# A ring of five tiles instead of four for the transposed query factor xT

## The chip, the core and the metric

The kernel runs on one core of one Trainium2 chip. The metric is the time of one execution on the device in microseconds (us), the median of three runs. Engines are named as the profile names them: PE is TensorE's matrix multiplications, PEld its weight loads, DVE is VectorE, ACT is ScalarE, POOL is GpSimd, SP is SyncE, which issues all the transfers (DMAs) of this kernel on one queue.

## The reference

Three stages follow one another. The first is a recurrence over 768 time steps, for 4 batches and 8 heads, with a 40x40 state each. The second is a dense layer pair with an ELU between, the third a mixture of eight experts whose gate is normalised over rows and columns.

```python
for t in range(S):                                   # B, H, S, D = 4, 8, 768, 40
    y[:, :, t] = einsum('bhd,bhde->bhe', rt, state)
    Sa = einsum('bhde,bhe->bhd', state, at)
    state = state * wt[:, :, None, :] - einsum('bhd,bhe->bhde', Sa, bt)
    state = state + einsum('bhd,bhe->bhde', vt, kt)

h = x @ w_in                                         # x: 3072 x 320, w_in: 320 x 2048
g = where(h > 0, h, exp(minimum(h, 0)) - 1)
x = g @ w_out

P = exp(x @ w_gate - max)                            # 8 experts
for _ in range(8): P /= P.sum(1); P /= P.sum(0); P *= N / E
for e in range(8): out += P[:, e] * (maximum(x @ w1[e], 0) @ w2[e])
```

## The kernel before, in words

**Stages.** The recurrence is cut into 24 chunks of 32 steps. The dense layer pair works on 12 blocks of 256 rows, each in 16 units of 128 hidden columns, and a block needs the output of two chunks. The units of the dense pair are woven between the pieces of the recurrence, so both run in the first 825 us or so; the experts follow until the end, with PE multiplying nearly without a gap.

**Order.** The program order on PE, DVE, ACT and POOL is fixed by hand: two strings of tokens in `PLAN` (`order2` for the first two passes, `order` from then on) name what each pass of the loop at L1238 records, and `pin_since` chains the instructions of each engine in that order. A token such as `E2+3` in the pass c means `E2` for chunk c + 3, and `m` is one unit of the dense pair. A pass therefore works on several chunks at once: `O3b` finishes the output of chunk c - 1, `E2` and `E1` prepare chunk c + 3, `H2` and `H3` carry the recurrence over chunk c. The SP queue is not pinned, and its transfers stand in an order that the scheduler has set; it issues them one after the other, and a transfer that must wait holds up those behind it.

**The tile xT.** `E2` (L369) transposes the factor of a chunk on PE into PSUM bank 2 (L374), and ACT copies it to the tile `xT` in SBUF (L376, shown in the profile as L469, the helper `cp`). `O3b` (L585) reads that tile four passes later: DVE multiplies the chunk's output into it in place (L598), POOL duplicates its last 64 columns (L599), and SP stores it to DRAM as `yd` (L603). `xprep` (L607) loads `yd` back as `yt` (L615), and PE transposes it for the dense pair (L621). The tiles of `xT` come from the pool `r2` (on the right side of SBUF) under one tag, and they are used in turn: with a ring of four, the copy for chunk c + 3 writes into the tile of chunk c - 1, so it waits for the store L603 of chunk c - 1. In a pass of `order` the store of chunk c - 1 and the copy of chunk c + 3 belong to neighbouring tokens: `O3b+-1 ... H1 ... E2+3`.

**What stands around the copy.** On ACT, in program order: the two activations of a dense unit (L640, L641), the copy of xT, four copies of the solved values to `VU` (`H2x`, L516), then the rounding `gh` of the next unit (L649), L640 and L641 again, and the copies of `KB` (`E1`, L469). On PE: the transposes of `E2` (L374), the multiplications of `H2` (L510), a second half of a unit (L665 to L669), the first half of another (L638), the transposes of `E1` (L365), which write banks 2 and 3, and the multiplications of `H3` (L534), which read `VU`. `E1` reads the tile `KE` of the same chunk, whose one buffer is then loaded again (L315) and scaled on POOL in `prep` (L355), and `E3` (L383) reads the result on PE.

**Pairs of passes.** Every other pass also ends a triangular solve for two chunks (`tsolve`, L418): its DVE steps L445 and L452 end shortly before `O3b`, and then SP issues eight stores `Td` (L460), eight loads `TT` (L464) and one load `LT` (L408) around the store L603. In the pass between, SP has none of these to issue at that place.

Of the kernel before, what the change touches and what calls it, by code (L numbers as in the profile page):

```python
# [9 lines left out]
F32 = mybir.dt.float32  # L10
# [103 lines left out]
def build(ctx, tc, r, k, v, w, a, b, w_in, w_out, wg, w1, w2, wa_d, kb_d, re_d, ro_d, vt_d, wp_d, consts, out, C, off):  # L114
# [63 lines left out]
    r2 = rec.enter_context(tc.tile_pool(name="r2", bufs=2, side="right"))  # L178
# [178 lines left out]
    def unpad(dst, ps):  # L357
        return dst.rearrange("p (j g e) -> p j g e", j=2, g=NG), ps.rearrange("p (g x) -> p g x", g=NG)[:, :, 0:128].rearrange("p g (j x) -> p j g x", j=2)[:, :, :, 0:D]
# [9 lines left out]

    def E2(c):  # L369
        z = st[c]  # L370
        z.xT = r2.tile([128, 384], F32, tag="xT", name="xT", bufs=4)
        xv = z.xC
        for g in range(NG):
            T.transpose(PS["E2"][0][:, 128 * g:128 * g + HR], xv[0:HR, g, :], ident[0:HR, 0:HR])  # L374
        o, i = unpad(z.xT[:, 0:DM], PS["E2"][0])
        cp("XT", 0, o, i)  # L376
# [91 lines left out]
    def cp(n, i, out, in_):  # L468
        (A.copy if PLAN["eng"][n][i] == "A" else G.tensor_copy if PLAN["eng"][n][i] == "G" else V.tensor_copy)(out=out, in_=in_)  # L469
# [661 lines left out]
    with ExitStack():  # L1131
# [37 lines left out]
        mg = msteps()  # L1169
        wgen = [(k, i) for i in range(NF1) for k in "io"]  # L1170
        fns = dict(ld=loads, ldw=loadw, ldk=loadk, lu=loadv, lv=loads2, prep=prep, H1=H1, H2=H2, H3=H3, H4=H4, E1=E1, E2=E2, E3=E3, E4=E4, T=tsolve, O1=O1, O2=O2, O3a=O3a, O3b=O3b, YW=YW, LT=LT)
        done = {("ld", 0), ("ld", 1)}

# [140 lines left out]
```

## Time and profile before

| what | value |
|---|---|
| median of three runs | 2249.49 us (2245.49 to 2250.47) |
| the profiled execution's own time | 2250.63 us |
| its span, first to last instruction | 2248.8 us |
| mean granted TensorE clock | 0.964 of full speed |
| PE busy | 2137.9 us, 95% |
| PEld busy | 1934.8 us, 86% |
| DVE, ACT, POOL busy | 928.5, 815.0, 439.7 us (41%, 36%, 20%) |

The page gives shares over the whole span. Some 1420 us of it are the experts, after 825 us. The change touches the first part alone, so the stretch from 270 to 750 us, where the passes of `order` repeat, says more than the shares do. [...]

### The profile page before, as it was taken

To read this page: it belongs to the slowest core of one execution; us is meant where nothing else is said; L and a number is where in the kernel's file an instruction comes from. 1 tells how busy PE (TensorE), PEld (TensorE's weight loads), DVE (VectorE), ACT (ScalarE), POOL (GpSimd) and SP (SyncE) were. 2 spreads that over 40 slices of the span, in tenths; PEclk is the share of its full clock that TensorE was granted. 3 is DMA by queue.
4 is the path that set the end of the run, shared out by engine and by line. 5 is a ranking of instruction groups with operands and counts; after the bars stand their busy time and mean duration, and the time that the engine had idled before them with its cause. 6 is when DMAs were issued, how large, how long until landed. Compare 5 with 4: busy or idle time off the path is not lost.

```text
span 2248.8 us, 48229 instructions
## 1 busy us (share of the span) xinstructions
PE 2137.9 (95%) x20483; PEld 1934.8 (86%) x20483; DVE 928.5 (41%) x1889; ACT 815.0 (36%) x1813; POOL 439.7 (20%) x545
## 2 busy tenths in 40 slices
PE   3788999999999999999999999999999999999998
PEld 2677888999898989898888888888888888888888
DVE  6686667777766322532222222222222222222222
ACT  2344555555544565223224324223224212112111
POOL 2354333443433261002002002002002002001000
PEclk9676999999999999999999999999999999999999
DMA  6654434344442142002113112002002001000000
GB/s 161 165 161 107 114 102 100 95 110 111 105 105 72 45 122 56 29 1 56 20 20 75 23 32 78 26 27 78 27 26 65 1 1 52 1 1 20 24 24 25
DMA packets 216657, 138.50 MB, mean 62 GB/s; under 512 B 143793, under 2 KB 192306, under 8 KB 216434
## 3 DMA queue, kind: packets, MB, share of 16 engines
q1 hardware_dynamic: 216434, 135.34, 22.9%
q8 instruction: 162, 2.65, 0.5%
q14 instruction: 61, 0.50, 0.1%
HBM read 116.80 MB, written 18.48 MB: 60 GB/s over the span
## 4 chain that ended last, share of the span: by engine, by line
PE 79%; DVE 9%; DMA 4%; issue 2%; ACT 2%; SPq 2%; POOL 1%; DVEq 0%; ACTq 0%; POOLq 0%
PE h L874 28%; PE pa L918 10%; PE pa L919 10%; PE pa L917 10%; PE ph L638 5%; PE h L863 2%; PE a L665 2%; DVE Wk L452 2%; DVE Tt L445 2%; DMA yd<-xT 1%; PE P L534 1%; PE a L666 1%; PE a L667 1%; PE P L383 1%; PE P L510 1%
## 5 line engine op out<-in xcount | busy, mean ns | idle before, releaser
L878 DVE SCALAR_TENSOR_TENSOR hl<-h,hh 128x512 fp32r<-128x512 f32 x384 | 265.3, 691 | 765.9 <-ACT hh L877 765.4
L877 ACT ACTIVATE hh<-h 128x512 fp32r<-128x512 f32 x384 | 229.6, 598 | 899.2 <-PE h L874 897.5
L874 PE MATMUL h<-xs,a 128*128 128x512 f32 x2280 | 547.0, 394 | 0.2 <-DVE hl L878 0.2
L874 PEld LDWEIGHTS h<-xs,a 128*128 128x128 f32 x2280 | 421.0, 188 | 109.8 <-issue 25.4
L918 PE MATMUL pa<-a,hl 128*128 128x320 f32 x1536 | 475.8, 310 | 0.8 <-DVE hl L878 0.8
L919 PE MATMUL pa<-a,hh 128*128 128x320 f32 x1536 | 475.2, 309 | 0.0
L917 PE MATMUL pa<-a,hh 128*128 128x320 f32 x1536 | 473.9, 309 | 0.3 <-ACT logits L692 0.3
L918 PEld LDWEIGHTS pa<-a,hl 128*128 128x128 f32 x1536 | 288.9, 188 | 6.7 <-DVE hl L878 1.7
L917 PEld LDWEIGHTS pa<-a,hh 128*128 128x128 f32 x1536 | 288.6, 188 | 5.2 <-ACT logits L692 0.4
L919 PEld LDWEIGHTS pa<-a,hh 128*128 128x128 f32 x1536 | 289.0, 188 | 0.0
L825 POOL TENSOR_TENSOR a<-rw,a 128x384 fp32r<-128x384 f32 x64 | 65.2, 1019 | 1057.5 <-ACT a L823 1044.4
L638 PE MATMUL ph<-X,Wt 128*128 128x256 f32 x1536 | 234.8, 299 | 8.2 <-DVE g L647 7.8
L651 POOL TENSOR_TENSOR gl<-g,gh 128x256 fp32r<-128x256 f32 x192 | 150.1, 782 | 385.1 <-ACT gh L649 305.0
L638 PEld LDWEIGHTS ph<-X,Wt 128*128 128x128 f32 x1536 | 212.2, 205 | 13.1 <-DVE g L647 11.5
L647 DVE SCALAR_TENSOR_TENSOR g<-m,ph 128x256 f32<-128x256 f32 x192 | 79.9, 416 | 205.0 <-ACT m L641 147.9
L928 DVE SCALAR_TENSOR_TENSOR acc<-pa,Pg,acc 128x320 f32<-128x320 f32 x168 | 81.0, 544 | 184.1 <-PE pa L919 184.1
L649 ACT ACTIVATE gh<-g 128x256 fp32r<-128x256 f32 x192 | 80.1, 417 | 163.5 <-DVE g L647 162.7
L452 DVE TENSOR_TENSOR Wk<-Wk,Tt 128x132 f32<-128x132 f32 (+24 forms) x279 | 109.4, 392 | 8.6
L874 PE MATMUL h<-X,a 128*128 128x512 f32 x456 | 108.9, 394 | 0.0
L640 ACT ACTIVATE m<-ph 128x256 f32<-128x256 f32 x192 | 73.0, 380 | 89.5 <-PE ph L638 86.4
L874 PEld LDWEIGHTS h<-X,a 128*128 128x128 f32 x456 | 84.1, 188 | 21.9 <-issue 5.0
L445 DVE TENSOR_TENSOR Tt<-Wk,LT 128x132 f32<-128x132 f32 (+24 forms) x279 | 90.1, 323 | 8.0
(189 smaller groups left out, 2700.3 us busy)
## 6 DMA issues: line engine op xcount, KB each, us to landing
LT<-Ad SPq DMA_DIRECT2D x22, 512.0 KB
rw<-in_moe_w SPq DMA_DIRECT2D x64, 160.0 KB
WA<-in_wa SPq DMA_DIRECT2D x23, 422.9 KB
KE<-in_kb SPq DMA_DIRECT2D x23, 416.0 KB
rw<-in_moe_w SPq DMA_DIRECT2D x64, 128.0 KB
VU<-in_vt SPq DMA_DIRECT2D x24, 320.0 KB
raw<-in_wp SPq DMA_DIRECT2D x16, 384.0 KB
rchk<-in_wp SPq DMA_DIRECT2D x16, 384.0 KB
```

Source lines behind the costliest of these rows:

```text
L445: V.tensor_tensor(out=tv, in0=Wk[:, :, 0:ni, j:j + 1].to_broadcast(sh), in1=LT2[:, :, j, j + 1:C].unsqueeze(2).to_broadcast(sh), op=ALU.mult,)
L452: V.tensor_tensor(out=Wk[:, :, 0:ni, j + 1:C], in0=Wk[:, :, 0:ni, j + 1:C], in1=tv, op=ALU.subtract)
L638: T.matmul(ph, lhsT=Wt[0:kp, wi, 128 * f:128 * f + 128], rhs=X[0:kp, xi, :], start=(i == 0), stop=(i == 7))
L649: A.activation(out=gh, in_=g, func=AF.Copy)
L651: G.tensor_tensor(out=gl, in0=g, in1=gh.bitcast(F32), op=ALU.subtract)
L874: T.matmul(h, lhsT=a1[:, wi, :], rhs=X[bk][:, xi, :], start=(i == 0 and n == 8), stop=(i == n - 1), skip_group_check=(n == 7))
L877: dve["hh"] = A.activation(out=hh, in_=h, func=AF.Relu)
L878: V.scalar_tensor_tensor(out=hl, in0=h, scalar=0.0, in1=hh.bitcast(F32), op0=ALU.max, op1=ALU.subtract)
L917: T.matmul(o, lhsT=hh[:, ts_], rhs=a2[:, 0, :], start=(f == 0), stop=False)
L918: T.matmul(o, lhsT=hl[:, ts_], rhs=a2[:, 0, :], start=False, stop=False)
L919: T.matmul(o, lhsT=hh[:, ts_], rhs=a2[:, 1, :], start=False, stop=(f == NF2 - 1))
L928: V.scalar_tensor_tensor(out=at, in0=o, scalar=Pg[:, tt, e:e + 1], in1=at, op0=ALU.mult, op1=ALU.add)
```

## The change

One number: the tag `xT` gets five buffers. The copy for chunk c + 3 then writes into the tile of chunk c - 2.

```diff
 def E2(c):
     z = st[c]
-    z.xT = r2.tile([128, 384], F32, tag="xT", name="xT", bufs=4)
+    z.xT = r2.tile([128, 384], F32, tag="xT", name="xT", bufs=5)
     xv = z.xC
```

The order of the instructions on all five engines stays as it was, the SP queue's too. The lists of semaphores that instructions wait for differ. This is the place on ACT where chunk 11's copy stands, with what stands around it (`ph` is a PSUM tile of the dense pair, `P_101` is bank 2, `DMAHW` are the semaphores of transfers):

```order
 L640 ACTIVATE m<-ph 128x256 [waits PE_49]
 L641 ACTIVATE m<-m 128x256 [waits Activation_49]
-L469 COPY xT<-P_101 128x320 [waits DMAHW5_49,PE_49,Pool_49]
+L469 COPY xT<-P_101 128x320 [waits DMAHW3_49,PE_49]
 L516 ACTIVATE VU<-P_100 32x320 [waits DMAHW4_49,PE_49]
```

The copy still names a transfer, but another one: the store of the chunk that held the tile five chunks ago. The wait for POOL (L599 of the chunk four before) is gone. Each tile takes 1536 bytes of a partition, so the pool `r2` grows by as much.

## Rows read from the trace of the kernel before

**Rows 1.** The page: busy time, share of the span, instructions.
```profile
PE 2137.9 (95%) x20483; PEld 1934.8 (86%) x20483; DVE 928.5 (41%) x1889; ACT 815.0 (36%) x1813; POOL 439.7 (20%) x545
```

**Rows 2.** Waits of PE, 270 to 750 us: total us, times, longest.
```profile
PE P L365 <- ACT xT L469: 13.3, 6, 2.9
PE P L481 <- issue: 3.1, 2, 1.8
...
PE P L534 <- ACT VU L516: 1.0, 5, 0.2
```

**Rows 3.** Waits of ACT, 270 to 750 us.
```profile
ACT xT L469 <- DMA yd<-xT: 29.4, 7, 5.3
```

**Rows 4.** Timeline of ACT at chunk 11's copy: start, us, instruction, idle before.
```profile
331.11 0.43 ACT L469 COPY xT<-P 128x320 f32<-128x320 f32 x1 [4.57 <-DMA yd<-xT]
331.56 1.77 ACT L516 ACTIVATE VU<-P 32x320 f32<-32x320 f32 x4
```

**Rows 5.** Timeline of PE at the same place.
```profile
325.95 1.13 PE L510 MATMUL P<-RH,TT 64*64 64x40 f32 x32
...
328.07 1.12 PE L638 MATMUL ph<-X,Wt 128*128 128x256 f32 x8
331.58 0.93 PE L365 MATMUL P<-cst,KE 104*128 104x104 f32 x8 [2.40 <-ACT xT L469]
...
344.21 1.13 PE L383 MATMUL P<-aB,KE 104*64 104x64 f32 x32
```

**Rows 6.** Timeline of SP's queue, 325 to 346 us: start, us to issue, transfer.
```profile
325.30 0.61 SPq L408 DMA_DIRECT2D LT<-Ad  x1
326.01 0.54 SPq L603 DMA_DIRECT2D yd<-xT  x1
326.67 3.80 SPq L464 DMA_DIRECT2D TT<-Td  x4
...
331.02 0.46 SPq L615 DMA_DIRECT2D yt<-yd  x1
331.58 0.35 SPq L327 DMA_DIRECT2D rO<-in_ro  x1
332.55 0.33 SPq L315 DMA_DIRECT2D KE<-in_kb  x1
```

**Rows 7.** The chain that ended last: start, us, what.
```profile
0.75 4.29 DMA WA<-in_wa
...
326.01 4.99 DMA yd<-xT
...
696.75 5.00 DMA yd<-xT
```

**Rows 8.** Timeline of PE one pass later (chunk 12's copy).
```profile
360.63 1.12 PE L638 MATMUL ph<-X,Wt 128*128 128x256 f32 x8
361.59 0.88 PE L365 MATMUL P<-cst,KE 104*128 104x104 f32 x8
```

**Rows 9.** Whole passes: us, busy PE, PEld, DVE, ACT, POOL; PEclk, DMA share, GB/s.
```profile
325.51:358.07 32.56, 29.39 (x517) 27.82 (x515) 21.47 (x51) 15.70 (x41) 11.72 (x14) 0.95 0.46 125
387.56:420.33 32.77, 29.51 (x517) 27.84 (x515) 22.50 (x55) 16.15 (x42) 11.71 (x14) 0.95 0.48 129
482.90:511.34 28.44, 28.26 (x523) 27.16 (x522) 20.18 (x46) 16.85 (x44) 12.20 (x15) 1.00 0.33 77
511.34:544.51 33.17, 30.85 (x517) 29.46 (x515) 21.68 (x52) 15.91 (x41) 11.71 (x14) 0.90 0.45 124
573.33:604.09 30.76, 28.21 (x517) 26.54 (x516) 21.50 (x51) 15.72 (x41) 11.69 (x14) 1.00 0.51 135
633.21:667.02 33.81, 30.66 (x517) 29.44 (x516) 21.40 (x51) 15.79 (x41) 11.73 (x14) 0.90 0.46 121
```

**Rows 10.** The same view, stretches at half clock.
```profile
446.70:450.10 3.40, 3.40 (x19) 3.40 (x18) 0.00 (x0) 0.82 (x3) 0.73 (x1) 0.50 0.35 54
518.40:525.20 6.80, 6.61 (x82) 6.54 (x83) 1.85 (x3) 3.60 (x11) 3.46 (x4) 0.50 0.39 115
702.70:709.60 6.90, 6.90 (x89) 6.57 (x88) 0.42 (x1) 3.66 (x11) 1.46 (x2) 0.51 0.19 62
```

**Rows 11.** Timeline of POOL at the same pass.
```profile
340.76 2.35 POOL L355 TENSOR_TENSOR KE<-KE,F 104x512 f32<-104x512 f32 x2
```

## The prediction

> **What bounds the kernel now.** I read the page first: PE is busy 95% of the span and ACT 36% [rows 1]. That share mixes the experts, where PE has hardly a gap, with the first 825 us, so I asked for the waits of PE in the passes that repeat, 270 to 750 us. Most of what PE waits for there is one thing: the transposes of E1 (L365) wait six times, 13.3 us in all, for ACT's copy of xT, and H3 (L534) five times, 1.0 us in all, for the VU copies that stand behind that copy on ACT [rows 2]. The next largest item is 3.1 us at L481 without a named cause. The same view for ACT says what the copy itself waits for: the store of the tile to DRAM, 29.4 us in seven waits [rows 3]; an eighth, before 270 us, brings the profile's count to eight.
>
> Chunk 11 shows one such wait in full. The store L603 is issued at 326.01, behind the stores and loads of the solve, and lands 4.99 us later [rows 6, 7]. The copy starts at 331.11 after 4.57 us of idle ACT [rows 4]. That the store is the cause is seen twice: SP's load of yt, which needs the same store, leaves at 331.02 [rows 6]. PE has gone on meanwhile with a dense unit, until 328.07 + 1.12 = 329.19, and then stands for 2.40 us, since L365 writes the PSUM bank that the copy reads [rows 5]. One pass later there is no solve to issue, the copy does not wait, and L365 follows L638 with no gap [rows 8]. So every other pass is long: 32.56 to 33.81 us, against 28.44 us in the best short one [rows 9].
>
> A second loss comes after the wait. [...] Its price stands in the passes: the one at 573 us has the same 517 matmul records as the other long ones and a clock of 1.00, and PE is busy 28.21 us in it. In the four others PE is busy 29.39, 29.51, 30.85 and 30.66 us for the same records, at clocks of 0.90 to 0.95 [rows 9].
>
> **The change, part by part.** No instruction is added, removed or moved; the SP queue keeps its order. What goes is the wait of the copy for the newest store. It now waits for the one a pass earlier, issued some 30 us before, and that store has long landed.
>
> *Stalls of PE.* With the copy at about 326.5 us, right after L641, the VU copies (1.77 us [rows 4]) follow H2, which ends at 327.08, and are done near 328.9. PE reaches L365 at 329.19, so both its wait and that of L534 disappear: 13.3 + 1.0 = **14.3 us** [rows 2]. For the wait before 270 us I count nothing; PE is held there by another transfer.
>
> *Clock.* If PE no longer stands, I expect the half clock to go too, as in the pass at 573 us. Above 28.21 us the four passes hold 1.18, 1.30, 2.64 and 2.45 us; for the fifth, at 702 us, whose stretch is as long as that at 518 us, I take 2.5. That is **10.1 us**. The bounds are nothing (the clock drops anyway) and half of the time spent at half clock, near 13.7 us: the stretches of 6.80 and 6.90 us [rows 10], a third of 6.8 us taken for the pass at 633 us, whose clock is the same as at 511 us, and two of 3.4 us taken for the passes at 0.95 [rows 9].
>
> [...]
>
> *What is late next.* PE then runs 2.40 + 0.2 + 1.18 = 3.8 us earlier in chunk 11's pass (0.2 is a fifth of L534's 1.0). Three loads stand behind the store on SP: yt, rO, KE. SP still waits until 331.0 for the store to land before it issues yt, so they hardly move: KE can go at about 331.95 instead of 332.55 [rows 6]. POOL scales KE at 340.76 without having waited for it [rows 11], so the load took at most 340.76 - 332.55 = 8.2 us; the nearest row with a landing is WA, 4.29 us [rows 7] and nearly of the same size. With 4.29 it lands at 336.2, before POOL wants it at 340.76 - 3.8 = 337.0. With 8.2 it lands at 340.15, 3.2 us late; L383 on PE has 344.21 - 340.76 - 2.35 = 1.1 us to spare [rows 5, 11], so PE would stand 2.1 us, in six passes (chunk 23 has no such load) 12.6 us. I take the row that is nearest, WA, and count **1 us** in all for the passes where PE gains most. The yt loaded here is the second of its block; its transposes come in the second half of the pass, so it costs nothing. The solve on DVE and its stores and loads follow PE's order and move with it, so H2 finds TT as it does now.
>
> *Space.* The 1536 bytes shift the addresses of tiles; I price that at nothing, no row of the trace tells of addresses.
>
> The sum is 14.3 + 10.1 - 1 = 23.4 us. The experts start earlier by that, and as PE is the bound there, nothing fills it again. From the profiled execution, 2250.63 us, this makes 2227.2; it lies 1.1 us above the median of the runs, so I give **2226 us**. What a measurement of this kernel can tell from no change is about 0.2%, 4.5 us.
>
> **The rivals.**
>
> *The stalls go, the clock does not come back.* At 446.7 us the clock is halved for 3.40 us where no copy of xT had waited before it [rows 10]; the two nameless stalls at L481 [rows 2] show that other gaps do this too. Then 14.3 us remain: 2236 from the profiled time, 2235 for the median.
>
> *KE takes the place of the store.* SP, held by the landing of yd, is then what PE waits for by way of POOL. Priced above at 12.6 us at most: 24.4 - 12.6 = 11.8 us, 2238. It decides from a load of about 336.97 + 1.1 - 331.95 = 6.1 us on. For it speaks that the store took 4.99 us in that crowd; against it that in the short pass nothing of the kind appears [rows 8, 9].
>
> *Nothing measurable.* ACT is busy 36% and PE 95% [rows 1]; if both rivals above hold at once, 24.4 - 10.1 - 12.6 = 1.7 us are left, 2248. [...]
>
> *Slower.* [...] The stall at L481 has no cause in the profile but "issue" [rows 2], 1.3 to 1.8 us, and the clock falls after it (1.7 us for the 3.40 us of [rows 10]), so about 3.3 us each time. Should it come in each of the 14 passes between 270 and 700 us instead of two, that costs 12 x 3.3 = 39.6 us against 23.4: 2266. It decides from seven more passes on. Against it: the short passes hold no pause now, and the one at 482.9 us is busy 28.26 of 28.44 us [rows 9].
>
> That the change does not do what it says would need a tile of five chunks ago to be late too; a store that left 30 us earlier is not.
>
> **How the numbers follow.** The forecast (18 to 28 us gained) has 0.62, the clock that stays low 0.17, KE 0.07, nothing measurable 0.09, slower 0.05. All of the first three are faster by more than 0.2%: 0.86; the same 0.09; slower 0.05. The range must hold 8 in 10: the forecast with its bounds and the rival of the clock, with the KE case at its edge. Below it goes to 14.3 + 13.7 and a little for the first wait, 2220; above to the KE case and the spread of the runs, 2240.
>
> **What would show it.** In the changed kernel's profile: no row of ACT's copy waiting for yd, and none of L365 waiting for the copy; passes of some 29 us in turn, all alike; PE busy near 28.2 us in each, with a clock of 1.00. The store itself should still take 4 to 5 us, and SP still wait for it ahead of yt. Wrong I would be if L365 or L534 waited for something else at the same place, if L383 waited for POOL's KE, or if stretches at half clock were as many as before.

## The result and the profile after

The changed kernel takes 2222.78 us, the median of five runs (2220.81 to 2225.52), against 2249.49 us (2245.49 to 2254.44, five runs): 26.7 us less, a ratio of 0.988 with a 95% interval of 0.9863 to 0.9897. The profiled execution took 2223.81 us with a span of 2221.9 us. The mean granted clock of the whole span, 0.964 before and 0.976 now, says little of the change: much of the difference lies in the first 260 us, where the clock is 0.79 and 0.86 and lies anywhere between 0.79 and 0.91 in the ten profiles of this case. From 260 to 760 us it is 0.96 before and 0.98 now (columns as in [rows 9], before and then after):

```profile
260.00:760.00 500.00, 472.83 (x8362) 449.71 (x8350) 334.15 (x797) 262.50 (x674) 183.93 (x228) 0.96 0.39 99
260.00:760.00 500.00, 485.53 (x8749) 462.69 (x8746) 340.66 (x810) 276.00 (x710) 191.13 (x236) 0.98 0.40 100
```

The page's first part, which answers to [rows 1], shows PE with 15.8 us less of busy time for the same 20483 instructions. The share went from 95% to 96%, so it would have told little.

```profile
PE 2122.1 (96%) x20483; PEld 1921.1 (86%) x20483; DVE 925.3 (42%) x1889; ACT 814.1 (37%) x1813; POOL 439.4 (20%) x545
```

The waits of PE, from 270 to 740 us (columns as in [rows 2]). The rows of L365 for ACT's copy and of L534 for VU are gone, and what is left is small, apart from L481, whose stalls were there before. The 1.4 us of L621 are new:

```profile
PE P L481 <- issue: 4.9, 3, 2.1
PE P L564 <- DVE X L626: 1.9, 8, 0.5
PE ph L638 <- DVE g L647: 1.7, 7, 0.3
PE P L621 <- DVE Am L385: 1.4, 4, 0.4
...
PE P L383 <- POOL KE L355: 0.3, 1, 0.3
```

ACT's copy waits for no transfer any more in the whole span. The one row of it among the waits of ACT is for the transposes that it copies (compare [rows 3]):

```profile
ACT xT L469 <- PE P L374: 2.9, 6, 1.2
```

Chunk 11 again, now some microseconds earlier. The timeline of ACT: the copy starts at once, and the VU copies wait only 0.28 us for H2 (compare [rows 4]).

```profile
325.20 0.41 ACT L469 COPY xT<-P 128x320 f32<-128x320 f32 x1
325.89 1.78 ACT L516 ACTIVATE VU<-P 32x320 f32<-32x320 f32 x4 [0.28 <-PE P L510]
```

The timeline of PE: L638, L365 and L534 follow one another without a gap (compare [rows 5]).

```profile
326.83 1.12 PE L638 MATMUL ph<-X,Wt 128*128 128x256 f32 x8
327.79 0.88 PE L365 MATMUL P<-cst,KE 104*128 104x104 f32 x8
328.60 1.30 PE L534 MATMUL P<-VU,KB 64*40 64x40 f32 x64
...
338.53 1.15 PE L383 MATMUL P<-aB,KE 104*64 104x64 f32 x32
```

The queue of SP: the store itself is as slow as before. It leaves at 324.61, and SP issues the load of yt, which needs it, 4.98 us later (compare [rows 6]). Now only SP waits for it, with the loads that stand behind it there.

```profile
324.61 0.54 SPq L603 DMA_DIRECT2D yd<-xT  x1
...
329.59 0.34 SPq L615 DMA_DIRECT2D yt<-yd  x1
330.04 0.35 SPq L327 DMA_DIRECT2D rO<-in_ro  x1
330.43 0.37 SPq L315 DMA_DIRECT2D KE<-in_kb  x1
```

The passes (columns as in [rows 9]), a short one and then the five long ones of [rows 9]. These five of 30.76 to 33.81 us are now 28.06 to 28.82 us, at a clock of 1.00, and no longer than the short one:

```profile
295.11:324.27 29.16, 28.62 (x523) 27.10 (x522) 21.28 (x50) 16.91 (x44) 12.06 (x15) 1.00 0.35 83
324.27:352.68 28.41, 27.60 (x517) 26.30 (x515) 21.85 (x51) 15.68 (x41) 11.79 (x14) 1.00 0.52 143
...
382.37:411.19 28.82, 27.66 (x517) 26.30 (x516) 22.58 (x54) 15.85 (x41) 11.73 (x14) 1.00 0.54 143
503.23:532.00 28.77, 28.17 (x517) 26.54 (x515) 22.23 (x52) 15.72 (x41) 11.75 (x14) 1.00 0.55 143
560.96:589.42 28.46, 27.76 (x517) 26.41 (x515) 21.85 (x51) 15.72 (x41) 11.73 (x14) 1.00 0.53 144
618.61:646.67 28.06, 27.50 (x517) 26.23 (x516) 21.85 (x51) 15.72 (x41) 11.78 (x14) 1.00 0.52 146
```

The starts of these passes, set against those in [rows 9], show where the time is won. The changed kernel is 1.2 us ahead at the first long pass, 5.2, 8.1, 12.4 and 14.6 us at the next four, and 20.4 us at the end of the last.

Between 325 and 667 us one long pass is in neither list, that of chunk 15's copy. It won nothing; before, and then after:

```profile
451.44:482.89 31.45, 29.38 (x516) 27.87 (x515) 22.59 (x55) 16.06 (x41) 11.36 (x14) 0.95 0.47 130
442.72:475.43 32.71, 30.38 (x517) 28.99 (x516) 23.45 (x56) 16.17 (x42) 12.48 (x15) 0.90 0.45 126
```

There the copy had waited only 1.86 us for the store, and PE did not stand behind it at L365. So not every other pass took 32.56 to 33.81 us before, as the prediction has it: two were shorter, with 30.76 and 31.45 us.

The same view for the two places between 270 and 700 us where the clock still falls. Each stands at a stall of L481, of 1.53 us up to 437.10 and of 2.13 us up to 468.56:

```profile
436.50:440.50 4.00, 3.40 (x18) 3.35 (x19) 0.00 (x0) 0.61 (x2) 0.73 (x1) 0.61 0.28 45
467.50:475.00 7.50, 6.45 (x37) 6.36 (x38) 4.28 (x13) 1.92 (x6) 1.55 (x4) 0.54 0.23 75
```

### The profile page after: what moved, and what is told of

It reads as the page before. It is cut to its first block, busy times and chain, and to the rows that moved or that the text cites. A ratio compares the mean times of both kernels' runs of the same rounds, so it can differ in the third digit from the quotient of the medians.

```text
span 2221.9 us, 48228 instructions
## 1 busy us (share of the span) xinstructions
PE 2122.1 (96%) x20483; PEld 1921.1 (86%) x20483; DVE 925.3 (42%) x1889; ACT 814.1 (37%) x1813; POOL 439.4 (20%) x545
## 3 DMA queue, kind: packets, MB, share of 16 engines
q8 instruction: 162, 2.65, 0.5%
## 4 chain that ended last, share of the span: by engine, by line
PE 76%; DVE 13%; DMA 4%; issue 3%; ACT 2%; SPq 1%; POOL 1%; DVEq 0%; ACTq 0%; POOLq 0%
PE h L874 28%; PE pa L918 10%; PE pa L919 10%; PE pa L917 10%; PE ph L638 5%; DVE Wk L452 3%; DVE Tt L445 3%; PE h L863 3%; PE a L665 1%; DVE g L647 1%; PE P L510 1%; PE a L666 1%; PE a L667 1%; PE P L383 1%; DMA KE<-in_kb 1%
## 5 line engine op out<-in xcount | busy, mean ns | idle before, releaser
L638 PE MATMUL ph<-X,Wt 128*128 128x256 f32 x1536 | 229.8, 294 | 9.2 <-DVE g L647 8.3
L638 PEld LDWEIGHTS ph<-X,Wt 128*128 128x128 f32 x1536 | 207.4, 200 | 13.5 <-DVE g L647 10.5
```

The lines of the kernel that those rows point to most:

```text
L638: T.matmul(ph, lhsT=Wt[0:kp, wi, 128 * f:128 * f + 128], rhs=X[0:kp, xi, :], start=(i == 0), stop=(i == 7))
```

## Experiments

My theory: the copy on ACT stands until the newest store has landed, PE stands behind ACT, and the clock falls after that. The rivals were that moved addresses make the gain, that the readers on DVE and POOL hold the tile too, that the moment or the place of the copy matters in some other way, and that the store costs something besides this wait. The first four experiments start from the kernel before, the last four from the changed one.

**1. The space without the tile.** The pool grows by the same 1536 bytes, but the ring stays at four.

```diff
     def E2(c):
-        z = st[c]
+        z = st[c]; c or G.memset(r2.tile([128, 384], F32, tag="pad", name="pad", bufs=1)[:, 0:1], 0.0)
```

> Ring of four, and a tile of 1536 bytes a partition that nothing uses is added to the same pool (one memset of one column on POOL). If the wait of the copy of xT for the newest store is what the change takes away, nothing changes: about 2249 us, and the copy still waits some 32 us for the store. If the gain came from the moved addresses of the pool, the time is near 2223 us with the waits still there or shorter.

Measured: 2250.39 us, ratio 1.0002 (0.999 to 1.0014). The waits are all there. The first row below is PE's from 260 to 760 us, the second ACT's over the whole span:

```profile
PE P L365 <- ACT xT L469: 13.6, 6, 2.7
```

```profile
ACT xT L469 <- DMA yd<-xT: 33.4, 8, 5.6
```

So more space in the pool does nothing by itself. The rival of the addresses is out, as far as this one way of shifting them goes.

**2. A tile of its own for the output.** The product no longer overwrites xT, so the store holds another tile.

```diff
-        y = x if c else mt.tile([128, 384], F32, tag="yt", name="yt", bufs=2)
+        y = r2.tile([128, 384], F32, tag="yo", name="yo", bufs=2) if c else mt.tile([128, 384], F32, tag="yt", name="yt", bufs=2)
```

> Ring of four, but O3b writes its product into a tile of its own (a ring of two) and stores that one; xT is free again after the two DVE products. If it is the landing of the store that holds the tile, the copy waits for nothing and the time is that of the change, 2220 to 2227 us. If the fifth tile is needed because the readers on DVE and POOL are late too, L365 still waits for the copy and the time stays within 5 us of 2249 us. The new ring of two puts DVE's product behind the store of two chunks before, which has landed by then: nothing for that.

Measured: 2222.05 us, ratio 0.9875 (0.9856 to 0.9894), the time of the change. With a ring of four, xT is free early enough once only the DVE products read it. Neither ACT's copy nor L365 shows a wait for the tile from 260 to 760 us. The new tile takes over both the store and POOL's column copy, so this run alone does not tell which of the two held xT; in experiment 4 POOL's copy still reads xT, and the wait is gone with the store.

**3. The copy later in the pass.** One token of `order` moves; no tile is added.

```diff
-... p m E2+3 p p p p lv G prep+4 H2 m m E1+3 ldk+4 prep+4 H3 m m x prep+4 ...
+... p m p p p p lv G prep+4 H2 m m E1+3 ldk+4 prep+4 H3 m m x E2+3 prep+4 ...
```

> Ring of four, with the token E2+3 moved from before E1+3 to the place before the third step of prep, some 8 us later in each pass; no more space. If only the moment of the copy against the landing of the store matters, the store has landed by then, no engine waits for it, and the time is that of the change within 6 us: 2220 to 2230 us (the transposes and the copy may now meet other work). If the order of the two transposes in bank 2 matters more than the wait, PE waits at the new place and the time is 2235 us or more.

Measured: 2225.44 us, ratio 0.9901 (0.9883 to 0.992). Nothing waits for the store; the transposes at the new place meet the copies of KB that E1 has left to ACT in the same bank. The waits of PE from 260 to 760 us:

```profile
PE P L374 <- ACT KB L469: 1.6, 5, 0.4
```

The ring of four was too short only for the place that the copy had.

**4. The store on another queue.** From chunk 5 on, ACT issues the store.

```diff
-            SY.dma_start(out=yd[c], in_=y)
+            (A if c > 4 else SY).dma_start(out=yd[c], in_=y)
```

> Ring of four, the store of the product issued on ACT's queue from chunk 5 on instead of SP's, so that it is not behind the solve's stores and loads. If the wait is made by the place in SP's queue (the store leaves 4.5 us after its data is ready) and by the crowd of transfers there, the store leaves some 4 us earlier and lands in 2 to 3 us, the copy does not wait, and the time is 2220 to 2232 us; ACT may lose some time to its wait for POOL's last column copy. If ACT standing for that wait costs as much as the wait before, the time is 2240 us or more.

Measured: 2222.66 us, ratio 0.9888 (0.9867 to 0.991). In the timeline of ACT the store leaves at 320.66, where SP had sent it at 326.01 in a pass that began at nearly the same time [rows 6]; the copy then waits for nothing:

```profile
320.66 0.37 ACTq L603 DMA_DIRECT2D yd<-xT  x1
321.07 0.49 ACT L469 COPY RH<-P 128x160 f32<-128x160 f32 x2 [2.07 <-PE P L481]
...
325.53 0.41 ACT L469 COPY xT<-P 128x320 f32<-128x320 f32 x1
```

ACT does stand for POOL's column copy ahead of the store. Its waits from 260 to 760 us:

```profile
ACT RH L469 <- POOL xT L599: 11.5, 10, 2.0
...
ACT RH L469 <- DMA Td<-Wk: 5.1, 2, 2.7
```

These 16.6 us cost nothing that can be measured, since no row of PE's waits names the copy of RH: here a wait on ACT counted only where it reached PE. Experiments 2 to 4 remove the same wait in three other ways, and the gain of each has an interval that overlaps that of the fifth tile.

**5 to 7. Putting the delay back.** In the changed kernel, spare copies on ACT ahead of the copy of the odd chunks from 9 on: 3, 8 or 14. They write into the tile that the copy then overwrites. No transfer is involved.

```diff
-        xv = z.xC
+        xv = z.xC; [A.copy(out=z.xT[:, 0:192], in_=cst[:, 0:192]) for _ in range(3 if c > 8 and c % 2 else 0)]
```

> The change, with three spare copies of 128x192 on ACT ahead of the copy of xT for the odd chunks from 9 on (about 1 us each time, eight times; they write into the tile that the copy then overwrites). If PE has room until it reaches L365 and L534, nothing is to be seen: within 4 us of the change, 2219 to 2228 us. If the sum of ACT's work is what counts, it costs 8 us: near 2231 us.

> The same with eight spare copies, about 2.6 us each time. PE should stand for some 1.2 us at L365 and L534 together, eight times: 10 us, so near 2233 us if the clock stays, and near 2243 us if each such stall also brings the half clock.

> The same with fourteen spare copies, about 4.5 us each time, as long as the wait for the store was. If PE's stall behind the copy, and the half clock after it, made the whole difference, the time is back: 2243 to 2254 us, with L365 waiting 2 to 3 us for the copy each time and stretches at half clock after most of them. If the store itself, or its wait on SP, was part of the price, the time stays 8 us or more below that of before: under 2241 us.

Measured: 2224.31 us (ratio to before 0.9891, 0.9871 to 0.9911), 2234.54 us (0.9933, 0.9913 to 0.9954) and 2258.49 us (1.0049, 1.003 to 1.0068). Against the change that is 1.5, 11.8 and 35.7 us more. With 3 copies PE shows no row of L365 or L534 for ACT from 260 to 760 us. With 8 it shows these:

```profile
PE P L365 <- ACT xT L469: 4.8, 7, 0.8
...
PE P L534 <- ACT VU L516: 1.5, 7, 0.2
...
PE P L510 <- ACT xT L372: 1.3, 1, 1.3
```

With 14 these, and below them the spare copies themselves in ACT's timeline:

```profile
PE P L365 <- ACT xT L469: 22.4, 8, 3.1
...
PE P L534 <- ACT VU L516: 1.1, 5, 0.2
```

```profile
324.19 5.33 ACT L372 COPY xT<-cst 128x192 f32<-128x192 f32 x14
```

The delay of the copy was free at first (1.5 us of time with 3 copies) and then went into PE's time (11.8 us with 8, 35.7 us with 14). The third run missed its figure: I had taken 0.32 us for a spare copy, but fourteen take 5.33 us, 0.38 each, so the delay was longer than the wait for the store (4.57 us [rows 4]), and PE stood for 23.5 us where it had stood for 14.3 us. It shows more than a return to the old time. The time rises by 35.7 us for 23.5 us of stalls, so 12 us come on top of the stalls. The clock is enough for that. It was 0.98 from 260 to 760 us in the change; with 14 copies it is:

```profile
260.00:760.00 500.00, 464.87 (x8172) 441.51 (x8170) 330.19 (x792) 295.64 (x772) 181.52 (x223) 0.95 0.38 96
```

A mean clock lower by 0.03 over 500 us is 15 us of full-speed time, and by the trace's clock records a stretch at half clock begins within 2.3 us of the end of each of the eight stalls at L365, which last 1.5 to 3.1 us. With 8 copies this hardly shows:

```profile
260.00:760.00 500.00, 480.47 (x8536) 455.86 (x8523) 338.26 (x807) 292.71 (x759) 189.32 (x233) 0.98 0.39 99
```

The mean clock is that of the change, and of the seven stalls at L365, of 0.3 to 0.8 us, one at most is followed by a half clock. The time, 2234.54 us, is the one expected if the clock stays. The three rows make 7.6 us of stalls for 11.8 us of time; the 4 us between them are not explained.

**8. KE ahead of the store's landing.** In the changed kernel, the load of yt goes behind the load of KE on SP.

```diff
-... p p m xl p m E2+3 ... H3 m m x prep+4 ...
+... p p m p m E2+3 ... H3 m m xl x prep+4 ...
-        SY.dma_start(out=z.KE[0:HR]..., in_=kb_d[c])
+        SY.dma_start(out=z.KE[0:HR]..., in_=kb_d[c]); first["KE"] = traced()[-1].name
-                SY.dma_start(out=yt, in_=yd[2 * blk + t])
+                SY.dma_start(out=yt, in_=yd[2 * blk + t]); t and tc.add_manual_dep(traced()[-1], first["KE"], ...)
```

> The change, with the second load of yt of a block put behind the load of KE on SP (and the token xl later in the pass), so that SP does not hold KE until the store has landed. The trace of the change shows the load of KE as what ends last there, with PE waiting for it once, 0.3 us. If KE is what is late next, up to 1 us a pass is won, 7 us in all at most and nearer 1 us: 2216 to 2224 us. If the issue stalls of PE and the clock bound it instead, it is the same as the change within 4 us. If the early KE load slows the store or the loads of the solve, it is slower by some us.

Measured: 2225.2 us, ratio to before 0.9897 (0.9877 to 0.9916): the same as the change. In the pass of chunk 11's copy KE now leaves ahead of yt, 4.75 us after the store, where it was 5.82 us in the change (330.43 less 324.61):

```profile
322.00 0.54 SPq L603 DMA_DIRECT2D yd<-xT  x1
...
326.75 0.32 SPq L315 DMA_DIRECT2D KE<-in_kb  x1
327.10 0.36 SPq L615 DMA_DIRECT2D yt<-yd  x1
```

KE does not come sooner for that. From its issue to POOL's start it is 8.06 us, where it was 5.66 us in the change, and POOL waits 2.23 us for it in this pass:

```profile
334.81 2.32 POOL L355 TENSOR_TENSOR KE<-KE,F 104x512 f32<-104x512 f32 x2 [2.23 <-DMA KE<-in_kb]
```

From 260 to 760 us POOL's waits for KE are 4.1 us in all, against 4.2 us in the change, and PE stands behind POOL for 1.7 us:

```profile
PE P L383 <- POOL KE L355: 1.7, 2, 1.0
```

So this run did not take the wait for KE away, and what a kernel without it would take stays open. It shows that the order of the two loads on SP is worth nothing that can be measured. None of these versions is faster than the change by more than its interval.

## Why the prediction was right

The forecast was 2226 us, and 2222.78 us was measured; the gain was 26.7 us where 23.4 us had been summed.

*The stalls of PE, 14.3 us.* Right. Both rows are gone, and the copy follows L641 as the prediction had it. Experiments 2 to 4 show that the landing of the store was the cause, and experiments 5 to 7 that ACT's delay costs PE time with no store in it.

*The clock, 10.1 us.* Right in kind, a little small in size: between 260 and 760 us the clock records of the two traces add up to 41.0 us at half clock before and 17.1 us after, which is 12.0 us of full-speed time. With the 14.3 us this makes 26.3 of the 26.8 us between the two profiled executions. The five stretches that followed the waits are all gone, 13.6 us, near the upper bound of 13.7, and the four passes of [rows 9] that had 0.90 to 0.95 are at 1.00; against that the stretch after L481 at 477 us before, 468 us now, grew from 3.4 to 6.8 us. The mark of 28.21 us of busy PE, above which I priced the passes, was not the floor: the five long passes of the change hold 27.50 to 28.17 us for the same 517 records. With stalls behind ACT again the half clock came back in experiment 7: 0.95 against 0.98 from 260 to 760 us, and a half clock within 2.3 us of each of its eight stalls at L365. It did not come each time: the pass at 573 us had its wait, 1.62 us, and a clock of 1.00. Which pass is spared differs between executions: in experiment 1 the pass near 580 us loses its clock and the one near 330 us keeps it.

*KE, 1 us.* Of the right order. POOL does wait for it now, as the row for the same pass shows, and PE stood for it 0.3 us once:

```profile
336.09 2.39 POOL L355 TENSOR_TENSOR KE<-KE,F 104x512 f32<-104x512 f32 x2 [1.07 <-DMA KE<-in_kb]
```

The 1.07 us is inside the slack of 1.1 us that the prediction had found ahead of L383. From WA's 4.29 us I had it land before POOL wants it; from its issue at 330.43 to POOL's start at 336.09 it took up to 5.66 us, between the two bounds and under the 6.1 us from which it would have decided. In the other kernels without the wait for the store PE stood longer for POOL's KE from 260 to 760 us: 2.1, 2.9 and 2.6 us in experiments 2, 3 and 5, and 1.7 us in experiment 8, which did not remove the wait.

*Space, nothing.* Right, by experiment 1.

*The rivals.* The stalls without the clock (2235), KE (2238), nothing measurable and the slower case did not come. The stalls at L481, from which the slower case was built, did not spread: three are in the view above instead of two, but the third, at 726 us, stood at 752 us before, just outside the view to 750 us.

## What to carry to other kernels

Make a ring long enough for the last reader of the tile, and count a store as a reader until it has landed: here ACT's copy waited 29.4 us in seven waits for it [rows 3], and with the fifth buffer not at all. The store lay behind other transfers in a queue and then took 3.8 to 5.1 us itself. Where the bound engine shows a repeated stall behind an engine that is idle two thirds of the time, follow the wait to its end before looking at shares. Here it hung on a tile's release, and a longer ring, a tile of its own for the output, a later place for the writer and another queue for the store each took it away, at 2222 to 2225 us. Price the stall with the clock that it loses (here 14.3 us of stalls and 12.0 us of clock), and look for what is late next with its slack, since that tells whether the gain stays.

## What the runs showed of the hardware

The price of a stall of PE was larger than the stall: in experiment 7, 35.7 us of time for 23.5 us of stalls, with the mean granted clock at 0.95 instead of 0.98 from 260 to 760 us. Of the stalls between 1.2 and 2.1 us, which one is followed by a half clock could not be told from the length. In the kernel before, PE stood for 1.62 us at L365 in the pass at 573 us, whose clock is 1.00 throughout [rows 9]:

```profile
579.41 0.93 PE L365 MATMUL P<-cst,KE 104*128 104x104 f32 x8 [1.62 <-ACT xT L469]
```

In the changed kernel a shorter stall, at L481, is followed by a stretch at half clock. Its row in PE's timeline, and that stretch (columns as in [rows 9]):

```profile
725.98 0.26 PE L481 MATMUL P<-Yw,aE 40*32 40x40 f32 x3 [1.20 <-issue]
```

```profile
727.20:730.70 3.50, 3.50 (x20) 3.50 (x19) 0.42 (x1) 1.15 (x3) 0.51 (x1) 0.54 0.41 96
```

Experiment 1 has both within one execution, at L365 behind ACT's copy. The stall of 2.07 us that ends at 333.6 us is not followed by a half clock, the one of 1.95 us that ends at 582.0 us is:

```profile
333.60:341.00 7.40, 6.62 (x107) 6.05 (x108) 3.19 (x7) 5.96 (x16) 3.87 (x5) 1.00 0.47 143
581.90:589.00 7.10, 7.02 (x89) 6.70 (x90) 1.84 (x3) 3.93 (x11) 3.47 (x4) 0.53 0.50 137
```

The stalls of PE at L481, with no cause in the profile but "issue", are still there, 4.9 us in three between 270 and 740 us, each a gap among matrix multiplications of one line. The pass of chunk 15's copy has the longest of them, 2.13 us, and a clock of 0.54 in the stretch at 467.5 us above. No run tried to remove these stalls, and no row names their cause. In the traces of the kernel before and of the changed one, three stalls at L481 stand at the same places in PE's order of multiplications and weight loads, about the 12 995th, the 14 019th and the 23 235th. In these six cases PE goes on 1.28 to 1.41 us after a packet of 16 KB has landed on the queue that the page lists with 162 packets and 2.65 MB:

```profile
q8 instruction: 162, 2.65, 0.5%
```

So much the two traces show of the order in time. What PE waits for at L481 was not shown.
